# Two MLP pieces behind the last attention outputs, and one cast ahead of a silu, in a fused attention and MLP kernel

## The chip, the core and the metric

The kernel runs on one core of a Trainium2 chip. The metric is the device time of one execution in microseconds (us); it was 192.3 us before the change (median of 3 runs). Engines are named as in the profile: PE is TensorE (PEld its weight loads), DVE VectorE, ACT ScalarE, POOL GpSimd, SP SyncE, which here only issues DMAs.

## The reference

A linear attention with decay (RWKV5) over 4 batches, 8 heads, 768 steps and a head width of 48, followed by a two-layer MLP over the 3072 tokens. Cut to what is computed:

```python
for t in range(S):
    cur = einsum('bhd,bhe->bhde', u * k[t], v[t])
    y[t] = einsum('bhd,bhde->bhe', r[t], state + cur)
    state = w * state + einsum('bhd,bhe->bhde', k[t], v[t])
x = y.transpose(0, 2, 1, 3).reshape(3072, 384)
h = x @ w_in                  # 384 -> 2048
out = (h * sigmoid(h)) @ w_out    # 2048 -> 384
```

Inputs and output are float32.

## The kernel before

**Tiling.** The 768 steps are cut into 6 chunks of 128. A unit is one chunk of one batch: unit i has chunk i // 4 and batch i % 4, 24 units in all, worked on in pairs (i, i+1). Within a chunk the attention is matrix products: the tile T turns r and k of a unit (transposes on PE, L251), `decay_one` multiplies them with powers of w into rT and kT (DVE, L259), `product_halves` forms the products of kT and rT (PE, L351, name P), `masked_halves` masks them (DVE, L358, m), `sums` adds up k times v for the state (PE, L374, Q) from kc, a decayed copy of k, and v16, a 16-bit copy of v made by `cast_v` (ACT, L242). `state_first` (DVE L387, then casts s1h on ACT, L332) and `state_second` carry the state on. `outputs_halves` (PE, L424 and L433, Z) makes the outputs of a pair from rT16, a 16-bit copy of rT, the states and the masked products; `evict_halves` adds the bonus term and writes y16 (DVE, L305).

**The MLP.** It runs over chunks of 4 x 128 tokens. `turn_y_dma` turns y16 into xT by a DMA transpose on SP's queue (L455). A first-layer piece (`l1_mm`, L477, and `l1_silu`, L485 on ACT) makes 128 of the 2048 hidden columns for 512 tokens: three matmuls and a silu. A second-layer piece (`l2_mm`, L498) is four of the sixteen matmuls that make 128 tokens' outputs; after every fourth piece `store` copies the sums (ACT, L504) and SP writes them out (L508). First-layer pieces of a chunk need xT of all four of its units.

**Order.** Nothing is left to a scheduler: the instructions of each engine stand in the order of the code. The start is a list of words written out by hand (`order`, from L577). There a word L4.11 is the matmuls of a first-layer piece of chunk 0 and G4.11 its silu, v165 is `cast_v` of unit 5, T5, rT5 and kT5 turn and decay unit 5, Q4 P4 s1_4 m4 s2_4 Z4 z4 are the steps of the pair (4, 5), yT and xT turn y on PE and copy it on ACT, ku, ru, kc, vu, sd are POOL's products, and i_q and i_o are POOL's DMAs that load a group of the MLP's weights (`ld_win`, L83, `ld_wout`, L88). Group 3 of the first weights, which L4.12 and later pieces read, is loaded by i_q3.

From unit 6 on a loop (L610) goes over the pairs 6, 8, ..., 22. MLP pieces wait in a list, `fillers`, and `fill(n)` plays the next n of them between the attention's steps. A pair plays 4 (L626) between its sums and its outputs, 4 (L639) after the turns of the next pair, 2 ahead of each of two `cast_r`, and 4 (L647) at its end, 16 in all. The second pair of a chunk adds that chunk's 16 first-layer and 16 second-layer pieces to the list, right after its outputs. What is left is played behind the loop. In the last pair (22, 23) there is no next pair to turn; its outputs are turned by DMA and are followed by the second-layer pieces of chunk 4 that are left (7 of them), and then by the first layer of chunk 5.

PSUM has four banks for the MLP pieces, sums and outputs (tag `moe`, four buffers); a new tile takes over one of the four banks and waits for the last reader of the tile that held it.

Of the kernel before, what the change touches and what calls it, by code (L numbers as in the profile page):

```python
# [15 lines left out]
def kernel(  # L16
# [23 lines left out]
    NU = B * NCH  # L40
# [9 lines left out]
    def unit(i):  # L50
        return divmod(i, B)
# [24 lines left out]
    def load(i):  # L76
        if i >= NU:
            return
        for dst, src in ((rin, r), (kin, k), (vin, v)):
            ld(i, dst, src)  # L80
# [131 lines left out]
    def bonus_products(i):  # L212
        bonus_ku(i)
        bonus_rku(i)
# [10 lines left out]
    def decayed_k(i):  # L225
        nc.gpsimd.tensor_tensor(out=kc[i % NIN][:, :, 0:D], in0=kin[i % NIN][:, :, 0:D],  # L226
                                in1=lamH if unit(i)[0] else lamC, op=ALU.mult)

    def bonus_sum(i):
        L(i)["rku"] = wrk.tile([128, H], FP, name="rku")  # L230
        nc.vector.tensor_reduce(out=L(i)["rku"], in_=L(i)["rku_f"],  # L231
                                axis=mybir.AxisListType.X, op=ALU.add)

    def bonus_v(i):
        L(i)["vu"] = wrk.tile([128, H, D], FP, name="vu", bufs=4)
        nc.gpsimd.tensor_tensor(out=L(i)["vu"], in0=vin[i % NIN],  # L236
                                in1=L(i)["rku"].unsqueeze(2).broadcast_to([128, H, D]),
                                op=ALU.mult)
# [24 lines left out]
    def turn(i):  # L263
        turn_one(i, 0)
        turn_one(i, 1)

    def decay(i):
        decay_one(i, 0)
        decay_one(i, 1)
# [72 lines left out]
    def product_halves(i):  # L342
        a = next_att().rearrange("p j (e g c) -> p j e g c", e=2, g=NP)
        L(i)["a2"] = a
        for p in range(NP):
            for e in range(2):
                rT, kT = L(i + e)["rT"], L(i + e)["kT"]
                for x in range(2):
                    o0 = HC * x
                    for j, r0 in ((0, 0), (1, 64)):  # L350
                        nc.tensor.matmul(a[o0:o0 + HC, j, e, p, :],  # L351
                                         kT[r0:r0 + D, p, HC * x:HC * x + HC],
                                         rT[r0:r0 + D, p, HC * x:HC * x + HC],
                                         start=True, stop=True)

    def masked_halves(i):
        am = L(i)["am2"] = wrk.tile([128, 2, 2, NP, HC], F16, name="am")
        nc.vector.tensor_tensor(  # L358
            out=am.rearrange("p j e g c -> p (j e g) c"),
            in0=L(i)["a2"].rearrange("p j e g c -> p (j e g) c"),  # L360
            in1=maskH.unsqueeze(1).broadcast_to([128, 2 * H, HC]), op=ALU.mult)

    def sums(i):
        sc, b = unit(i)
        xs = range(2 if sc < NCH - 1 else 1)
        L(i)["sp"] = [ps.tile([128, 512], FP, name="sp", tag="moe", bufs=4) for _ in xs]
        for p in range(NP):
            for e in range(2):
                for x in xs:
                    rows = slice(HC * x, HC * x + HC)  # L370
                    for j in range(2):
                        h = 2 * p + j
                        c0 = (e * NP + p) * D
                        nc.tensor.matmul(L(i)["sp"][x][64 * j:64 * j + 64, c0:c0 + D],  # L374
                                         kc[(i + e) % NIN][rows, h, :],
                                         L(i + e)["v16"][rows, h, :],
                                         start=True, stop=True)
# [7 lines left out]
    def state_first(i):  # L385
        s1 = L(i)["s1"] = wrk.tile([PR, 2, NP, D], FP, name="s1")
        nc.vector.tensor_tensor(out=flat(s1), in0=L(i)["sp"][0][0:PR, 0:HD],  # L387
                                in1=flat(L(i)["sdec"]), op=ALU.add)
        spread_state(nc.scalar.copy, inner[i // 2 % 2], s1)

    def state_second(i):
        sc, b = unit(i)
        if sc == NCH - 1:
            return
        sd = wrk.tile([PR, 2, NP, D], FP, name="sd")
        nc.vector.tensor_tensor(out=sd, in0=L(i)["s1"], in1=w_half(), op=ALU.mult)
        nc.vector.tensor_tensor(out=flat(st[b // 2]), in0=L(i)["sp"][1][0:PR, 0:HD],
                                in1=flat(sd), op=ALU.add)
# [6 lines left out]
    def next_state(i):  # L405
        sc, b = unit(i)
        if sc == NCH - 1:
            return
        spread_state(nc.gpsimd.tensor_copy, carried_in(i + B), st[b // 2])
        decayed_state(i + B)  # L410

    def outputs_halves(i):
        yp = L(i)["y2"] = [ps.tile([128, 512], FP, name="yp", tag="moe", bufs=4)
                           for _ in range(2)]

        def place(e, x, c0, n):
            y0 = rows(e, x)
            return yp[e][y0:y0 + HC, c0:c0 + n]

        for p in range(NP):  # L420
            for e in range(2):
                for x in (e, 1 - e):
                    s = inner[i // 2 % 2] if x else carried_in(i)
                    nc.tensor.matmul(place(e, x, PW * p, PW),  # L424
                                     L(i + e)["rT16"][:, p, HC * x:HC * x + HC], s[:, e, p, :],
                                     start=(p == 0), stop=False, skip_group_check=True)
        for p in range(NP):
            for j in range(2):
                h = 2 * p + j
                for e in range(2):  # L430
                    for x in range(2):
                        r = HC * x
                        nc.tensor.matmul(place(e, x, D * h, D), L(i)["am2"][r:r + HC, j, e, p, :],  # L433
                                         L(i + e)["v16"][r:r + HC, h, :],
                                         start=False, stop=True, skip_group_check=True)

    def evict_halves(i):
        yp = L(i)["y2"]
        new_y(i)
        add_bonus(i, yp[0])  # L440
        new_y(i + 1)
        for x in range(2):
            y0 = rows(1, x)
            add_bonus(i + 1, yp[1], slice(HC * x, HC * x + HC), slice(y0, y0 + HC))
# [8 lines left out]
    def turn_y_dma(i):  # L453
        sc, b = unit(i)
        nc.sync.dma_start_transpose(out=x_tile(sc)[:, :, b, :],  # L455
                                    in_=L(i)["y16"].rearrange("p h d -> p (h d)"))
# [81 lines left out]
    def fill(n):  # L538
        for _ in range(n):
            if fillers:  # L540
                fillers.pop(0)()

    def second(sc):
        return [lambda b=b, p=p: l2(sc, b, p) for b in range(B) for p in range(4)]

    def rest_first(sc):
        return [lambda ft=ft: l1(sc, 2, 2, ft) for ft in range(0, NFT, 2)]

    def first(sc):
        return [lambda f=f: l1(sc, 0, B, f) for f in range(NFT)]  # L550
# [5 lines left out]
    def piece(word, f):  # L556
# [24 lines left out]
        v163 4*A23 vu2 i_q2 rd3 vu3 am2 am3 L0.0 G0.0 L0.2 G0.2 Y2 y162 Y3 y163 kc0 yT2 xT2 L0.4  # L581
        G0.4 kc1 yT3 xT3 L0.6 G0.6 S0 st0 kc2 T4 kT4 rT4 kc3 L2.0 G2.0 L2.2 G2.2 ku4 v164
        L2.4 G2.4 S2 L2.6 G2.6 st2 ru4 i_q3 r164 L4.8 G4.8 L4.9 G4.9 rd4 ku5 kc4 kc5 sd4
        L4.10 G4.10 T5 kT5 rT5 L4.11 G4.11 vu4 ru5 i_o0 v165 Q4 P4 s1_4 m4 rd5 s2_4 r165
        L4.12 G4.12 vu5 i_o1 L4.13 G4.13 Z4 z4 L4.14 G4.14 L4.15 G4.15 yT4 xT4
        yT5 xT5 T6 kT6 rT6 kc6 ku6 ru6 i_o2 H0 H1 v166 r166 H2 H3 T7 kT7 rT7 kc7 ku7 i_o3 v167
        r167 H4 ru7 rd6 sd6 vu6 sn4
# [22 lines left out]
    for i in range(B + 2, NU, 2):  # L610
        sc, b = unit(i)
        nxt = range(i + 2, min(i + 4, NU))
        sums(i)
        product_halves(i)
        state_first(i)
        state_second(i)
        masked_halves(i)
        if i == B + 2:
            bonus_sum(i + 1)
            bonus_v(i + 1)  # L620
        for n in nxt:
            bonus_products(n)
            decayed_k(n)
        if i > B + 2 or sc < NCH - 1:
            next_state(i)
        fill(4)  # L626
        outputs_halves(i)
        for n in nxt:
            turn(n)
        evict_halves(i)  # L630
        turn_y_dma(i)
        turn_y_dma(i + 1)
        if b:
            fillers.extend((first(sc) if sc > 1 else rest_first(sc)) + second(sc))
        for n in nxt:
            decay(n)
        load(i + B)
        load(i + 1 + B)
        fill(4)  # L639
        for n in nxt:  # L640
            bonus_sum(n)
            cast_v(n)
            bonus_v(n)
        for n in nxt:
            fill(2)
            cast_r(n)
        fill(4)  # L647
    fill(len(fillers))


# [28 lines left out]
```

## Time and profile before

| | us |
|---|---|
| median of 3 runs (191.97 to 192.69) | 192.3 |
| profiled execution | 192.8 |
| its span, first to last instruction | 191.0 |
| PE busy | 180.1 (94%) |
| POOL busy | 118.6 (62%) |
| DVE busy | 114.7 (60%) |
| ACT busy | 99.0 (52%) |
| granted TensorE clock, mean | 0.997 |

The profiled execution is 0.5 us above the median, and 1.8 us of it lie outside its span. Places in time are us from the span's start. A row of the timeline gives the start, the length from the first to the last end of the merged instructions, the engine, line, operation, tiles and number, and in brackets the idle time of the engine ahead of it and what ended it. Matmuls overlap, so the length of a row of them is a little more than the distance to the next row.

### The profile page before, as it was taken

The numbers are of one execution on the slowest core, as the hardware profiler recorded it, in microseconds if no ns is written. First come the engines' busy times: TensorE is split into PE (matmuls) and PEld (weight loads), VectorE is DVE, ScalarE is ACT, GpSimd is POOL, SyncE is SP. The second block draws the span as 40 slices with busy tenths as digits, with TensorE's granted clock in tenths as the row PEclk, the third lists the DMA queues.
The fourth block names the chain that finished last, engine by engine and source line by source line (L and its number), as shares of the span: only waits on it lengthen the run. The fifth ranks groups of instructions, "written<-read, shape, count | busy, mean of one in ns | idle before, by whom it ended". The sixth has DMA issues, their size and how long they took to land. (4 is left out here: it accounts for less than half of the span.)

```text
span 191.0 us, 6511 instructions
## 1 busy us (share of the span) xinstructions
PE 180.1 (94%) x2786; PEld 113.1 (59%) x2786; DVE 114.7 (60%) x189; ACT 99.0 (52%) x193; POOL 118.6 (62%) x151
## 2 busy tenths in 40 slices
PE   7798898998999999999999999999999999999993
PEld 2454783677666786655656655656646566444562
DVE  7578876845884794695686775766853944200120
ACT  5394477576433293158573178563267643289200
POOL 6499989699899977849649649749659130000000
PEclk9999999999999999999999999999999999999998
DMA  5999979999959469269177269177386202310022
GB/s 95 209 191 189 207 149 184 155 218 222 148 113 195 148 134 200 65 129 223 26 147 165 65 138 209 32 146 165 84 177 163 41 4 82 85 42 0 6 79 84
DMA packets 90272, 24.42 MB, mean 128 GB/s; under 512 B 83329, under 2 KB 90242, under 8 KB 90242
## 3 DMA queue, kind: packets, MB, share of 16 engines
q1 hardware_dynamic: 84992, 20.39, 49.1%
q0 software_dynamic: 3712, 3.15, 10.8%
q10 hardware_dynamic: 1538, 0.46, 1.1%
q8 instruction: 22, 0.36, 0.8%
q14 instruction: 8, 0.07, 0.1%
HBM read 20.65 MB, written 4.72 MB: 133 GB/s over the span
## 5 line engine op out<-in xcount | busy, mean ns | idle before, releaser
L477 PE MATMUL hps<-xT,win 128*128 128x512 f16 (+1 forms) x360 | 66.4, 337 | 1.0 <-DMA xT<-y 0.5
L485 ACT ACTIVATE gT<-hps 128x512 f16<-128x512 f32 x96 | 55.8, 597 | 17.4 <-PE hps L477 14.2
L498 PE MATMUL ops<-wout,gT 128*128 128x384 f16 x368 | 62.5, 326 | 0.0
L477 PEld LDWEIGHTS <-win 128*128 128x128 f16 x360 | 33.8, 98 | 26.8 <-issue 1.6
L498 PEld LDWEIGHTS <-gT 128*128 128x128 f16 x368 | 35.2, 98 | 23.4
L236 POOL TENSOR_TENSOR vu<-vin,rku 128x384 f32<-128x384 f32 x24 | 21.1, 892 | 21.0 <-DVE rku L231 21.0
L218 POOL TENSOR_TENSOR ku<-kin,u_bc 128x384 f32<-128x384 f32 x24 | 24.4, 1018 | 11.1 <-DMA kin<-in_k_dram 7.5
L504 ACT COPY osb<-ops 128x384 f32<-128x384 f32 x20 | 9.6, 479 | 41.7 <-PE ops L498 31.1
L305 DVE TENSOR_TENSOR y<-yp,vu 64x384 f16<-64x384 f32 (+1 forms) x34 | 18.9, 555 | 13.7 <-PE yp L433 5.0
L222 POOL TENSOR_TENSOR rku_f<-rin,ku 128x384 f32<-128x384 f32 x24 | 24.3, 1012 | 1.7
L226 POOL TENSOR_TENSOR kc<-kin,lamH 128x384 f16<-128x384 f32 x20 | 20.7, 1038 | 0.0
L259 DVE TENSOR_TENSOR kT<-att,lamK 112x512 f32<-112x512 f32 x24 | 16.4, 683 | 4.8 <-PE att L251 4.8
L387 DVE TENSOR_TENSOR s<-sp,sdec 112x384 f32<-112x384 f32 x10 | 5.6, 558 | 22.0 <-PE sp L374 20.7
L259 DVE TENSOR_TENSOR rT<-att,lamR 112x512 f32<-112x512 f32 x24 | 16.5, 686 | 2.5 <-PE att L251 1.1
L332 ACT CAST s1h<-s 48x384 f16<-48x384 f32 x20 | 10.2, 511 | 9.6 <-DVE s L387 9.5
L242 ACT CAST v<-vin 128x384 f16<-128x384 f32 x24 | 11.5, 511 | 5.4 <-DMA vin<-in_v_dram 5.2
L506 DVE COPY osb<-ops 128x384 f32<-128x384 f32 x3 | 1.7, 558 | 20.6 <-issue 16.5
L273 DVE CAST rT<-rT 112x512 f16<-112x512 f32 x16 | 13.9, 906 | 0.0
L231 DVE TENSOR_REDUCE rku<-rku_f 128x8 f32<-128x384 f32 x24 | 12.5, 544 | 1.4 <-POOL rku_f L222 1.4
L358 DVE TENSOR_TENSOR am<-att,maskH 128x1024 f16<-128x1024 f32 x10 | 12.2, 1218 | 1.2 <-PE att L351 1.2
L351 PE MATMUL att<-rT,kT 48*64 48x64 f32 x640 | 11.6, 220 | 0.0
L251 PE MATMUL att<-ident,kin 64*112 64x64 f32 x192 | 9.4, 217 | 1.5 <-DMA kin<-in_k_dram 1.5
(74 smaller groups left out, 167.1 us busy)
## 6 DMA issues: line engine op xcount, KB each, us to landing
rin<-in_r_dram SPq DMA_DIRECT2D x24, 192.0 KB, 3.7
vin<-in_v_dram SPq DMA_DIRECT2D x24, 192.0 KB, 4.3
kin<-in_k_dram SPq DMA_DIRECT2D x23, 192.0 KB, 4.5
out_dram<-osb SPq DMA_DIRECT2D x23, 192.0 KB, 2.7
win<-in_moe_w_in_dram POOLq DMA_DIRECT2D x4, 384.0 KB, 6.5
wout<-in_moe_w_out_dram POOLq DMA_DIRECT2D x4, 384.0 KB, 6.2
xT<-y SPq DMA_TRANSPOSE x18, 2.3
kin<-in_k_dram ACTq DMA_DIRECT2D x1, 192.0 KB, 3.7
```

Source lines behind the costliest of these rows:

```text
L218: nc.gpsimd.tensor_tensor(out=L(i)["ku"], in0=kin[i % NIN][:, :, 0:D], in1=u_bc, op=ALU.mult)
L222: nc.gpsimd.tensor_tensor(out=L(i)["rku_f"], in0=rin[i % NIN][:, :, 0:D], in1=L(i)["ku"], op=ALU.mult)
L226: nc.gpsimd.tensor_tensor(out=kc[i % NIN][:, :, 0:D], in0=kin[i % NIN][:, :, 0:D], in1=lamH if unit(i)[0] else lamC, op=ALU.mult)
L231: nc.vector.tensor_reduce(out=L(i)["rku"], in_=L(i)["rku_f"], axis=mybir.AxisListType.X, op=ALU.add)
L236: nc.gpsimd.tensor_tensor(out=L(i)["vu"], in0=vin[i % NIN], in1=L(i)["rku"].unsqueeze(2).broadcast_to([128, H, D]), op=ALU.mult)
L259: nc.vector.tensor_tensor(out=L(i)[key].rearrange("p g (y t) -> p y g t", y=2), in0=L(i)["t"][0:PR, :, x], in1=lam, op=ALU.mult)
L273: copy(out=L(i)["rT16"], in_=L(i)["rT"])
L305: nc.vector.tensor_tensor(out=y16[a], in0=y[b, 0:HD], in1=vu[a], op=ALU.add)
L358: nc.vector.tensor_tensor(out=am.rearrange("p j e g c -> p (j e g) c"), in0=L(i)["a2"].rearrange("p j e g c -> p (j e g) c"), in1=maskH.un ...
L477: nc.tensor.matmul(hps[:, f, :], win[:, q, (ft + f) * 128:(ft + f + 1) * 128], xts[sc][:, q, b0:b0 + nb, :].rearrange("p b t -> p (b t)"), ...
L485: nc.scalar.activation(out=gts[sc][:, ft:ft + m, b0 * C:(b0 + nb) * C], in_=hpss[b0, ft], func=AF.Silu)
L498: nc.tensor.matmul(opss[b], gts[sc][:, ft, b * C:(b + 1) * C], wout[:, ft, :], start=(ft == 0), stop=(ft == NFT - 1))
```

## The change

Two edits. In the hand-written start, the cast of unit 5's v (v165) is moved on ACT's queue from behind the silu G4.11 (and behind POOL's i_o0 and ru5, to which it has no tie) to ahead of that silu. In the loop, the last `fill` of a pair plays 2 pieces in place of 4 from pair 20 on. For pair 20 that makes 14 pieces in place of 16; all later steps keep their numbers, so the two pieces come to stand behind the outputs of pair 22: nine second-layer pieces follow them in place of seven. For pair 22 itself it changes nothing, as the rest of the list is played right after. The order of POOL's instructions stays as it was. On SP's queue one store of chunk 4 moves from ahead of the last two DMA transposes to behind them, and on ACT one copy (L504) from ahead of the casts s1h of pair 22 to behind them.

```diff
-        L4.10 G4.10 T5 kT5 rT5 L4.11 G4.11 vu4 ru5 i_o0 v165 Q4 P4 s1_4 m4 rd5 s2_4 r165
+        L4.10 G4.10 T5 kT5 rT5 L4.11 v165 G4.11 vu4 ru5 i_o0 Q4 P4 s1_4 m4 rd5 s2_4 r165
...
         for n in nxt:
             fill(2)
             cast_r(n)
-        fill(4)
+        fill(4 if i < NU - 4 else 2)
     fill(len(fillers))
```

## The prediction

> **What bounds the kernel now.** I read the page's busy shares first, then the chain that ended last, then PE's waits in two stretches, then the timeline around each wait that the change touches.
>
> ```profile
> PE 180.1 (94%) x2786; PEld 113.1 (59%) x2786; DVE 114.7 (60%) x189; ACT 99.0 (52%) x193; POOL 118.6 (62%) x151
> ...
> PEclk9999999999999999999999999999999999999998
> ```
>
> PE is the bound: the other engines are busy at most 62% of the span and PE's clock is granted in full. The change adds and removes no PE work, so it can gain only idle time of PE. The chain that ended last, in order of time (start, length, what):
>
> ```profile
> 164.24 2.35 DMA xT<-y
> 166.59 0.14 issue
> 166.72 10.52 PE hps L477 x48
> 177.24 7.80 PE ops L498 x48
> ```
>
> The last transfer that turns y lands at 166.59, and behind it PE works through the first and second layer of the last chunk to the end. PE's own waits from 52 us to the end are a single row (waiter, releaser, total, times, longest), and from 28 to 52.5 us five:
>
> ```profile
> PE hps L477 <- DMA xT<-y: 0.5, 1, 0.5
> ```
>
> ```profile
> PE sp L374 <- ACT v L242: 1.1, 2, 0.9
> PE att L251 <- DMA kin<-in_k_dram: 0.5, 1, 0.5
> PE hps L477 <- DVE s L387: 0.5, 1, 0.5
> PE yp L424 <- ACT gT L485: 0.4, 1, 0.4
> PE yT L462 <- DVE y L305: 0.2, 1, 0.2
> ```
>
> So each edit aims at one wait: the pieces at the 0.5 us for xT, the cast at the 0.9 us for v16 of unit 5.
>
> **Edit 1, two pieces behind the last outputs.** PE's timeline there:
>
> ```profile
> 161.15 0.44 PE L433 MATMUL yp<-v,am 64*64 64x48 f16 x32
> 161.52 4.72 PE L498 MATMUL ops<-wout,gT 128*128 128x384 f16 x28
> 166.72 0.59 PE L477 MATMUL hps<-xT,win 128*128 128x512 f16 x2 [0.47 <-DMA xT<-y]
> ```
>
> 28 matmuls (seven pieces) take 4.72 us, 0.169 each, so a piece takes 0.67 and two take 1.35. Taken from ahead of the sums of pair 22, they let everything of that pair start 1.35 earlier: the outputs end at 160.17, the transposes land at 166.59 - 1.35 = 165.24. Nine pieces now last from 160.17 to 166.24, the same end as before, and xT has been there for 1.0 us. The idle 0.47 goes: gain 0.47.
>
> What else waits on pair 22, now that its cover is 1.35 shorter? From DVE's, ACT's and POOL's rows: rT16 of unit 23 is ready at 152.97 + 1.78 = 154.75 and is wanted at 160.69 - 1.35 = 159.34. The bonus term (POOL) ends at 154.47 and is wanted at 160.3. v16 ends at 153.12, wanted by the sums at 155.30. The chain that starts at the sums moves with them: the mask ran 158.14 to 159.36 and is wanted at 161.15, a slack of 1.8 that stays, because the four pieces between sums and outputs stay (16 matmuls, 2.77 us from 157.99, are the cover; without it the mask would cost PE about 1.0). The casts s1h end at 158.82 - 1.35 = 157.47, wanted at 159.34. The copy that now stands behind them on ACT (0.48) ends by 158.0; what waits for its bank is the second of the nine pieces, at 160.8. On SP's queue the store of one tile moves behind the two transposes; nothing waits for a store for the next 14 us, and the transposes have one transfer less ahead of them. The last copy of chunk 4 ends at about 166.8, and the bank it frees is wanted by the fourth first-layer piece, 166.24 + 3 x 0.66 = 168.2. All of this costs nothing. Bounds of edit 1: gain 0 (the wait reappears elsewhere) to 0.47; I take 0.47, since the nearest cover has 1.0 us to spare. Once the wait is gone nothing is late next: PE is bound by its own work from 52 us to the end.
>
> **Edit 2, the cast ahead of the silu.** ACT's and PE's rows:
>
> ```profile
> 29.92 1.57 ACT L485 ACTIVATE gT<-hps 128x512 f16<-128x512 f32 x3
> 32.21 0.60 ACT L485 ACTIVATE gT<-hps 128x512 f16<-128x512 f32 x1 [0.71 <-PE hps L477]
> 32.70 0.50 ACT L242 CAST v<-vin 128x384 f16<-128x384 f32 x1
> ```
>
> ```profile
> 32.10 0.22 PE L374 MATMUL sp<-v,kc 64*64 64x48 f16 x4
> 33.26 0.41 PE L374 MATMUL sp<-v,kc 64*64 64x48 f16 x28 [0.94 <-ACT v L242]
> ```
>
> v of unit 5 was issued at 24.23 and landed 5.1 us later, at 29.3. ACT is free from 31.49, so the cast (0.50) ends at 31.99, inside ACT's 0.71 idle, and G4.11 still starts at 32.21: no cost on ACT. On PE the sums of the pair run through at 32.10; locally 0.94 of idle goes.
>
> What is late next? P4 needs rT of unit 5, which DVE ends at 32.07 + 0.68 = 32.75, so PE stalls some 0.4 after the sums and P4 ends about 33.84 in place of 34.57: lead 0.73. L4.12 then needs weight group 3, issued at 27.41 and landed 6.7 later, at 34.1: its lead is only 0.4. But the outputs of the pair had waited 0.40 for G4.12, and ACT comes to that silu about 0.9 sooner, so PE gets the lead back there. DVE (mask, rku, state, y back to back from 34.75 to 39.2) and POOL (back to back from the bonus of unit 5, which waits for rku, at 36.53 to the state product at 45.89) run 0.7 earlier. So all three engines bring a lead of about 0.7 to unit 9's turn, where PE already waited for a load:
>
> ```profile
> 50.82 0.39 PE L251 MATMUL att<-ident,rin 64*112 64x64 f32 x8
> 51.67 0.44 PE L251 MATMUL att<-ident,kin 64*112 64x64 f32 x8 [0.46 <-DMA kin<-in_k_dram]
> ```
>
> k of unit 9 was issued at 43.7 and took 7.9 us to land, at 51.6. Neither end hangs on compute: SP's queue issues loads back to back from 40.3 to 47.6, and the sixteen DMA engines are full (DMA share 1.20 to 1.32 in every 2 us stretch from 38 to 50, and 0.29 from 52 to 54). PE will reach k's part of this turn near 50.5 and wait 1.2 us in place of 0.46. The lead is spent there, and from 52 us on everything stands as before.
>
> One thing can move that landing: the POOL instructions i_o1 to i_o3 sit in the chain that runs 0.7 earlier, and each loads 384 KB of weights on the other queue. The last of these was issued at 44.1 and landed 7.2 later, at 51.3, just ahead of k. While both queues have work the weights take more:
>
> ```profile
> q0 software_dynamic: 506, 0.38, 82.0%
> q1 hardware_dynamic: 1135, 0.21, 45.1%
> ```
>
> (47.5 to 50.5 us; packets, MB, share of 16 engines.) The same bytes go before k's last packet either way, and the engines are full, so I take 0 for the landing. Its bounds are 0.7 earlier (the weights' lead handed on in full) and, against me, 2.5 us later (one whole weight transfer put in front of it that was not there). Edit 2 is worth 0, between +0.7 and -2.5.
>
> The longer wait at unit 9's turn could cost more than itself through the clock. The trace grants 1.00 in the 2 us stretch from 32 to 34 that holds the 0.94 us idle, and 1.00 from 50 to 52, so I take no cost. The Trainium skill (TensorE: Matmul & The Clock Gate, What's actually happening) speaks against long PE waits: after an idle window of about 3.4 us the clock falls to half. By that rule 1.2 us is too short to trip it; had it tripped, a window at half clock would cost about 1.7 us, an estimate from that page alone.
>
> **Sum.** 0.47 + 0 = 0.47 of the profiled 192.8, that is 192.3, with a span of 190.5. The median stood 0.5 below the profiled execution; 192.3 - 0.47 gives 191.8, or -0.25%. A measurement of this kernel tells about 0.5% (0.96 us) from no change, so this falls within it.
>
> **Rivals.** (a) The load is not what holds 52 us: k of unit 9 lands 0.7 earlier with the weights, or is earlier anyway in executions without the profiler. Then both edits count, 0.47 + 0.7 = 1.2: 191.1 us, faster by 0.6%. For: only the last two of k's sixteen parts land after 51, when the DMA share has dropped to 0.2. Against: full engines up to then. (b) Slower: the weights push k of unit 9 back. Place: unit 9's turn; price: up to one weight transfer, the 2.5 us in which q0 dominates, less 0.47, so 194.3 us. It decides from a landing later than 51.62 + 0.47 + 0.96 = 53.05. For: the shares above. Against: the last weights already land before k, so no further bytes can get ahead. (c) Nothing: the wait for xT comes back as another of the same size at the last pair, 192.3. Against: 1.0 us of slack at the transposes, 1.8 at the mask.
>
> **Chances.** Forecast 0.71, (a) 0.15, (b) 0.07, (c) 0.07. The forecast and (c) lie within 0.5%, with 0.02 of the forecast's spread beyond it on the fast side: faster 0.17, same 0.76, slower 0.07. The three runs of before spread by 0.7, so the forecast alone reaches from 191.4 to 192.2. The range takes in (a) and most of (c): 191.0 to 192.5; (b) is left out.
>
> **What would show it.** Right: no wait of PE on xT near 166, the sums of pair 4 without a wait on v, PE's wait on k at unit 9's turn grown to about 1.2 us with its end still near 51.7, and the work behind it at unchanged places up to pair 22. Wrong: unit 9's turn ending below 51.2 (towards a) or above 52.5 (towards b), a wait at L424 or L433 of pair 22, or any new PE wait between 52 and 166 us.

## Result, and the profile after

The changed kernel is faster: median 191.38 us against 192.84 us before (20 executions of each; the 192.3 us ahead of the change is the median of the first three), ratio 0.9935 with a 95% interval of 0.9908 to 0.9962, that is 1.25 us (0.7 to 1.8). Ratios here and below leave out executions more than 1.5% above the fastest of their kernel, medians do not, so a ratio is not quite that of the medians. The forecast was 191.8 us and no measurable change; the time lies in the range, but at the place of rival (a), faster by 0.6%. The profiled execution took 190.8 us with a span of 189.0, 2.0 less than the one before.

The page after, busy shares and granted clock:

```profile
PE 179.4 (95%) x2786; PEld 112.8 (60%) x2786; DVE 115.0 (61%) x189; ACT 98.9 (52%) x193; POOL 118.7 (63%) x151
...
PEclk9999999999999999999999999999999999999999
```

The chain that ended last, its last long pieces in order of time (start, length, what):

```profile
158.92 5.96 PE ops L498 x36
164.87 10.36 PE hps L477 x48
175.23 7.80 PE ops L498 x48
183.03 2.65 PE ops L523 x32
```

Before, this chain began with the transfer that turns y; now PE's own work goes on behind it and the transfer is gone from its end. PE's waits after, first from 28 to 52.5 us, then from 52 us to the end:

```profile
PE hps L477 <- DVE s L387: 0.7, 1, 0.7
PE yT L462 <- ACT gT L485: 0.5, 1, 0.5
PE sp L374 <- ACT v L242: 0.2, 1, 0.2
```

```profile
PE yp L433 <- DVE am L358: 0.2, 1, 0.2
```

Both waits that the edits aimed at are gone. So is the wait on k of unit 9, which was forecast to grow. Behind 52 us one wait is new, that of L433 on the mask; ahead of it yT now waits for a silu where the outputs of pair 4 (L424) did before. The places, in PE's rows of the timeline after; first the last outputs and what follows them:

```profile
158.85 6.02 PE L498 MATMUL ops<-wout,gT 128*128 128x384 f16 x36
164.71 10.52 PE L477 MATMUL hps<-xT,win 128*128 128x512 f16 x48
```

36 matmuls, and then the first layer with no idle time in brackets. Next the sums of pair 4, on ACT and PE:

```profile
31.16 0.53 ACT L242 CAST v<-vin 128x384 f16<-128x384 f32 x1
...
31.89 0.44 PE L374 MATMUL sp<-v,kc 64*64 64x48 f16 x32
32.00 0.60 ACT L485 ACTIVATE gT<-hps 128x512 f16<-128x512 f32 x1 [0.31 <-PE hps L477]
```

The cast ends ahead of the sums, which are one row of 32 now, and the silu behind it still waits for PE, as worked out. Last, unit 9's turn:

```profile
49.83 0.39 PE L251 MATMUL att<-ident,rin 64*112 64x64 f32 x8
50.05 0.39 PE L251 MATMUL att<-ident,kin 64*112 64x64 f32 x8
```

k follows r with no wait. Why is seen on SP's queue, in the row that issues k of unit 9, before and then after:

```profile
43.73 0.62 SPq L72 DMA_DIRECT2D kin<-in_k_dram  x1
```

```profile
39.95 2.67 SPq L72 DMA_DIRECT2D kin<-in_k_dram  x1
```

and the time from this issue to its landing, from the answer on that tile after:

```profile
DMA to landing us min/median/max: 7.3/7.3/7.3
```

It was issued 3.8 us earlier and had landed at 47.3, where before it landed at 51.6. The cast can't have done that: SP's queue already stood one load further at 12 us, long ahead of the moved cast.

**Where the 2.0 us of span came from**, as the lead of the later trace over the earlier at the same step: 0.21 at the sums of pair 4 (32.10 to 31.89, before anything the change moves), 1.00 at unit 8's turn (50.33 to 49.33), 1.62 at k of unit 9 (51.67 to 50.05), 1.66 at the outputs of pair 8 (64.00 to 62.34), 1.38 at the sums of pair 10 and then without change up to pair 20 (142.87 to 141.50), 2.01 at the last chunk's first layer (166.72 to 164.71), 2.01 at the end. So the opening gave 0.21, the cast 0.79, the load's wait 0.66 with the outputs of pair 8, the new wait on the mask took 0.28, and the pieces gave 0.63.

### The profile page after: what moved, and what is told of

It is laid out like the page before. It is cut to its first block, busy times and chain, and to the rows that moved or that the text cites. A ratio compares the mean times of both kernels' runs of the same rounds, so it can differ in the third digit from the quotient of the medians.

```text
span 189.0 us, 6512 instructions
## 1 busy us (share of the span) xinstructions
PE 179.4 (95%) x2786; PEld 112.8 (60%) x2786; DVE 115.0 (61%) x189; ACT 98.9 (52%) x193; POOL 118.7 (63%) x151
## 4 chain that ended last, share of the span: by engine, by line
PE 71%; POOL 18%; issue 3%; DMA 3%; DVE 2%; ACTq 1%; ACT 0%; POOLq 0%; DVEq 0%
PE ops L498 31%; PE hps L477 26%; PE att L251 4%; POOL ku L218 4%; POOL kc L226 4%; PE att L351 4%; POOL rku_f L222 3%; POOL vu L236 3%; DMA u_bc<-in_u_dram 3%; PE yp L424 2%; PE yp L433 2%; PE sp L374 2%; POOL win L83 2%; PE ops L523 1%; POOL wout L88 1%
## 5 line engine op out<-in xcount | busy, mean ns | idle before, releaser
L485 ACT ACTIVATE gT<-hps 128x512 f16<-128x512 f32 x96 | 55.8, 597 | 18.9 <-PE hps L477 15.5
L504 ACT COPY osb<-ops 128x384 f32<-128x384 f32 x20 | 9.6, 478 | 40.3 <-PE ops L498 31.0
L305 DVE TENSOR_TENSOR y<-yp,vu 64x384 f16<-64x384 f32 (+1 forms) x34 | 18.9, 555 | 13.4 <-PE yp L433 5.6
L387 DVE TENSOR_TENSOR s<-sp,sdec 112x384 f32<-112x384 f32 x10 | 5.6, 557 | 19.2 <-PE sp L374 17.7
L242 ACT CAST v<-vin 128x384 f16<-128x384 f32 x24 | 11.4, 511 | 3.0 <-DMA vin<-in_v_dram 2.9
L351 PEld LDWEIGHTS att<-rT,kT 48*64 48x64 f32 x640 | 10.5, 135 | 0.2 <-DVE rT L259 0.2
## 6 DMA issues: line engine op xcount, KB each, us to landing
rin<-in_r_dram SPq DMA_DIRECT2D x24, 192.0 KB, 3.9
vin<-in_v_dram SPq DMA_DIRECT2D x24, 192.0 KB, 4.4
kin<-in_k_dram SPq DMA_DIRECT2D x23, 192.0 KB, 4.4
out_dram<-osb SPq DMA_DIRECT2D x23, 192.0 KB, 2.7
kin<-in_k_dram ACTq DMA_DIRECT2D x1, 192.0 KB, 3.5
```

What stands on the lines that cost most here:

```text
L305: nc.vector.tensor_tensor(out=y16[a], in0=y[b, 0:HD], in1=vu[a], op=ALU.add)
L351: nc.tensor.matmul(a[o0:o0 + HC, j, e, p, :], kT[r0:r0 + D, p, HC * x:HC * x + HC], rT[r0:r0 + D, p, HC * x:HC * x + HC], start=True, stop ...
L485: nc.scalar.activation(out=gts[sc][:, ft:ft + m, b0 * C:(b0 + nb) * C], in_=hpss[b0, ft], func=AF.Silu)
```

## The experiments

Each trace is read by stretches, since the opening ahead of the change moves much more than the change: the sums of pair 4 began between 31.9 and 36.3 us in the profiled executions of this case, whose instructions up to there differ only in the place of the cast and, in e12, of one weight load. All lengths are from the first matmul of one step to the first of another. "Pair 4 to k9" runs from the sums of pair 4 to k's part of unit 9's turn; "wait on k9" is the distance of k's part of that turn from unit 8's, less 0.45, which it is without a wait; "gap" is the distance between the last second-layer matmul ahead of the last chunk's first layer and that layer, less 0.16, which it is in an unbroken row; "k9 to end" goes to the last matmul.

| trace | cast ahead | pieces behind outputs | pair 4 to k9 | wait on k9 | gap | k9 to end |
|---|---|---|---|---|---|---|
| before | no | 7 | 19.57 | 0.62 | 0.64 | 135.79 |
| after | yes | 9 | 18.16 | 0 | 0 | 135.40 |
| e1_pieces | no | 9 | 18.94 | 0 | 0 | 135.39 |
| e2_cast | yes | 7 | 19.77 | 1.60 | 0.45 | 135.61 |
| e3_k9_first | no | 7 | 18.94 | 0 | 0.39 | 135.78 |
| e4_k9_first_cast | yes | 7 | 18.16 | 0 | 0.84 | 136.23 |
| e5_both_again | yes | 9 | 18.16 | 0 | 0 | 135.39 |
| e6_both_k9_first | yes | 9 | 18.14 | 0 | 0 | 135.40 |
| e7_k9_late | no | 7 | 20.40 | 1.44 | 0.37 | 135.52 |
| e8_k9_late_cast | yes | 7 | 20.68 | 2.50 | 0.69 | 137.52 |
| e9_cast_again | yes | 7 | 18.18 | 0 | 0.59 | 135.99 |
| e10_pieces_again | no | 9 | 18.96 | 0 | 0 | 135.74 |
| e11_fill6 | no | 5 | 18.96 | 0 | 2.14 | 137.53 |
| e12_q3_earlier | yes | 9 | 18.16 | 0 | 0 | 135.40 |

### One edit at a time

```diff
# e1_pieces, e10_pieces_again
-        fill(4)
+        fill(4 if i < NU - 4 else 2)
# e2_cast, e9_cast_again
-        ... L4.11 G4.11 vu4 ru5 i_o0 v165 Q4 ...
+        ... L4.11 v165 G4.11 vu4 ru5 i_o0 Q4 ...
```

**e1_pieces.** 

> Edit 1 alone (14 pieces in pair 20, so nine behind the last outputs; the cast of unit 5's v stays behind its silu). Theory A (PE idles 0.64 us start to start ahead of the last chunk's first layer, and nine pieces cover all of it): 0.6 us less than before, ratio 0.997; no wait of PE on xT near 166 us. Rival B (nearly the whole measured 1.25 us comes from this edit): 1.2 us less, ratio 0.9935. Rival C (the wait comes back at pair 22): no change.

Measured: 1.0005 (0.9970 to 1.0040), the time of before. In its trace the wait on xT is gone and from k9 to the end PE takes 135.39, which is 0.39 less than in e3_k9_first, the nearest trace with seven pieces. The stretch shows the mechanism of theory A, with 0.39 in place of 0.6, and excludes rivals B and C; the times exclude B, but can't resolve 0.4 us.

**e10_pieces_again**, the same kernel on another chip. 

> Edit 1 alone once more, on another chip. Theory A: 0.4 to 0.6 us less (the gap ahead of the last first layer measured 0.39 to 0.69 us beyond one matmul in the traces without the edit, and none in those with it), ratio 0.997 to 0.998. Rival C (no change): ratio 1.000 or above again.

Measured: 0.9994 (0.9967 to 1.0021). Again no gain to be seen in the time, and again no gap in the trace. But from k9 to the end this trace took 135.74, no less than e3: PE lost 0.35 within the outputs of pair 12, near 95 us, on nothing that the profile names. That PE has no gap is shown; that edit 1 alone makes the whole execution faster was not shown by these two comparisons, and the ratio that it should give, 0.997, lies at the lower edge of both intervals.

**e2_cast.** 

> Edit 2 alone (v of unit 5 is cast ahead of G4.11; pair 20 keeps 16 pieces). Theory A (PE, DVE and POOL gain 0.8 to 1.0 us by pair 6, and unit 9's turn hands most of it on because k of unit 9 has landed in most executions): 0.6 to 1.0 us less, ratio 0.995 to 0.997. Rival D, the step on record (k of unit 9 lands near 51.6 whatever the cast does, and takes the lead back): no change, with PE's wait on k at unit 9's turn near 1.2 us. In both PE's wait on v at the sums of pair 4 is gone and its wait on xT near 166 us stays.

Measured: 1.0012 (0.9976 to 1.0048), with executions from 191.3 to 195.1. Its profiled execution is the forecast's own case. The two longest of PE's waits from 28 to 54 us, and unit 9's turn:

```profile
PE att L251 <- DMA kin<-in_k_dram: 1.4, 1, 1.4
PE hps L477 <- DMA win<-in_moe_w_in_dram: 0.7, 1, 0.7
```

```profile
50.89 0.39 PE L251 MATMUL att<-ident,rin 64*112 64x64 f32 x8
52.72 0.44 PE L251 MATMUL att<-ident,kin 64*112 64x64 f32 x8 [1.44 <-DMA kin<-in_k_dram]
```

Here k of unit 9 landed 19.7 us after the sums of pair 4, in the trace before 19.5. The cast's lead is spent on that load to the last tenth: 19.77 from pair 4 to k9 with the cast, 19.57 without. L4.12 also waits for its weights, as foreseen.

**e9_cast_again**, on another chip. 

> Edit 2 alone once more, on another chip. Its first comparison gave 1.0012, with the load of k of unit 9 late in its profile (PE waited 1.4 us for it). Theory A (the lead counts when that load has landed, and how early it lands differs between executions and chips): somewhere from no change to 0.8 us less, ratio 0.996 to 1.000, with executions both near 191.5 and near 193.5. Rival H (edit 2 alone is worth nothing, and the two edits together do something that neither does): ratio 1.000 or above again, no fast group.

Measured: 0.9965 (0.9926 to 1.0003), six executions of 12 between 191.4 and 192.0. In its trace k of unit 9 had landed 16.1 us after the sums of pair 4, PE did not wait for it, and the stretch took 18.18. There is a fast group, which speaks for theory A and against rival H.

### The load taken out of the way

```diff
-    load(8)
-    load(9)
+    ld(9, kin, k)
+    ld(8, rin, r)
+    ld(8, kin, k)
+    ld(9, rin, r)
+    ld(8, vin, v)
+    ld(9, vin, v)
```

**e3_k9_first.** 

> The kernel before, with the loads of units 8 and 9 issued in another order: k of unit 9 first, then r and k of unit 8, r of unit 9, v of unit 8, v of unit 9 (same bytes). It takes the load out of unit 9's turn. Theory A (the load is late in some executions only): 0.2 to 0.4 us less, ratio near 0.9985, and the slower half of the executions comes closer to the faster. Rival D (the load is late in all executions): 0.5 to 0.7 us less, ratio 0.997. In both no wait of PE on k at unit 9's turn.

Measured: 0.9964 (0.9934 to 0.9994). No wait on k, 18.94 from pair 4 to k9: the same as in e1, e10 and e11, where the old order of loads did not make PE wait either. The interval holds what both theories expect; the traces decide for A.

**e4_k9_first_cast.** 

> The same new order of loads, with edit 2 (the cast ahead of G4.11) and without edit 1. With the load out of the way all theories say that the cast's lead is kept: against the same order of loads without the cast 0.8 to 1.0 us less (ratio to the kernel before 0.993 to 0.995). If it is less than 0.4, the lead is lost to something other than the load (a wait of DVE, POOL or PE between 34 and 52 us, or the mask of pair 8).

Measured: 0.9968 (0.9938 to 0.9998), no better than e3 in time, though the interval also holds part of what was expected. The stretch from pair 4 to k9 took 18.16, so the cast's lead, 0.78, is there up to unit 9. In this trace 0.45 of it went into a longer gap ahead of the last first layer (0.84, in e3 0.39): from the sums of pair 4 to the last matmul it took 154.39, and e3 154.72. Why the gap was longer, and why the times of these 12 executions show nothing, was not found.

**e6_both_k9_first**, both edits with that order. 

> Both edits with the new order of loads (k of unit 9 first). Theory A: both leads are kept in all executions, so 1.2 to 1.7 us less than before, ratio 0.991 to 0.994, and at or below the changed kernel. Rival F (the load order costs elsewhere what it saves, or the lead is lost at the mask of pair 8): no better than the changed kernel.

Measured: 0.9911 (0.9867 to 0.9954), median 191.35, beside 0.9930 of the changed kernel in the same comparison: the lowest ratio of the study, but not told apart from the changed kernel's. Its trace has the 18.14 and no gap.

**e5_both_again**, the changed kernel once more. 

> The changed kernel itself, once more, beside the kernel before on one chip. Theory A (edit 1 is worth 0.64 us in every execution; the cast's lead of about 0.8 us at unit 9's turn counts only where k of unit 9 has landed by then): 0.6 to 1.4 us less, ratio 0.993 to 0.997. Rival E (the opening before the change, which moves by 1 to 3 us from execution to execution, made most of the first comparison's 1.25 us): ratio 0.997 or above.

Measured: 0.9930 (0.9892 to 0.9968), the first result again, against another 23 executions of before. Rival E falls, if narrowly: the gain is not the opening's.

### The load made late

```diff
     load(8)
-    load(9)
+    ld(9, rin, r)
+    ld(9, vin, v)
+    for b in range(2):
+        spare = big.tile([128, H, D], FP, name=f"spare{b}")
+        nc.sync.dma_start(out=spare, in_=v[b, :, 0:C, :].rearrange("h t d -> t h d"))
+    ld(9, kin, k)
```

**e7_k9_late.** 

> The kernel before with k of unit 9 made late on purpose: its load is issued last of the six, behind two more loads of 192 KB into spare tiles that nothing reads. All theories: PE waits 1.5 to 3 us on it at unit 9's turn, ratio 1.005 to 1.012. It is the base for the next kernel.

**e8_k9_late_cast.** 

> The same late load with edit 2 (the cast ahead of G4.11). The step on record (the load takes the lead back) says: the same time as with the late load alone, within 0.2 us, and PE's wait on k longer by 0.7 to 1.0 us. Rival G (the lead reaches the end by another way, through DVE or POOL): 0.7 us or more less than with the late load alone.

Measured: 1.0104 (1.0050 to 1.0158) for the late load, and 1.0183 (1.0103 to 1.0263) with the cast, median 198.4 against 195.1 us (six executions each). Up to unit 9's turn the step on record holds: 20.40 without the cast, 20.68 with it, and PE's wait on k longer by 1.06. Rival G falls. But the cast made this kernel no faster, rather slower (the two intervals overlap), and the trace shows where time was lost. PE's row at unit 9's turn, and then 2 us stretches behind it (length, busy time and instructions of PE, PEld, DVE, ACT, POOL, granted clock, DMA share, GB/s):

```profile
55.55 0.44 PE L251 MATMUL att<-ident,kin 64*112 64x64 f32 x8 [2.34 <-DMA kin<-in_k_dram]
```

```profile
54.00:56.00 2.00, 0.46 (x9) 0.39 (x10) 1.52 (x3) 0.00 (x0) 1.92 (x3) 1.00 0.32 62
56.00:58.00 2.00, 2.00 (x7) 0.91 (x8) 1.75 (x3) 0.00 (x0) 1.92 (x3) 0.51 0.47 93
58.00:60.00 2.00, 2.00 (x9) 1.03 (x8) 1.84 (x3) 0.25 (x1) 1.94 (x4) 0.63 1.11 220
60.00:62.00 2.00, 2.00 (x15) 1.18 (x13) 0.00 (x0) 1.16 (x3) 1.92 (x4) 1.00 1.02 205
```

After a wait of 2.34 us PE's clock went to half, and came back within the stretch from 58 to 60 us: 7 and 9 matmuls started in 2 us, then 15. From k9 to the outputs of pair 8 PE took 14.02 us in place of the 12.34 of e7, 1.7 more. After waits of 1.28 (e7), 1.44 (e2) and 1.97 us (e11, below) the clock stayed at 1.00. The Trainium skill (TensorE: Matmul & The Clock Gate, What's actually happening) puts the fall to half clock behind an idle window of about 3.4 us; the fall is seen here, after less idle time than that. Nor does the length of one wait decide alone: in the opening of e11 the clock went to half near 11 us with no wait of PE above 0.53 us in the 7 us before (e3, e7, e8 and e12 show the same fall there):

```profile
12.00:14.00 2.00, 2.00 (x9) 0.60 (x6) 1.98 (x3) 1.97 (x6) 1.47 (x3) 0.50 1.04 206
```

To its last matmul the profiled execution of e8 took 3.5 us more than that of e7: 1.2 in the opening, up to the sums of pair 4, 0.3 up to unit 9's turn, 1.7 at half clock, and 0.3 in the gap ahead of the last first layer.

### The pieces the other way, and an earlier load of weights

```diff
# e11_fill6
-        fill(4)
+        fill(4 if i < NU - 4 else 6)
# e12_q3_earlier (on e6_both_k9_first)
-        L4.0 ... L2.2 G2.2 ku4 v164 ... st2 ru4 i_q3 r164 ...
+        L4.0 ... L2.2 G2.2 i_q3 ku4 v164 ... st2 ru4 r164 ...
```

**e11_fill6.** 

> The kernel before with 18 pieces in pair 20 in place of 16, so that five follow the last outputs: edit 1 the other way round. Theory A (the pieces behind the outputs cover the transposes one for one): the gap ahead of the last first layer grows from 0.4 to 0.7 by two pieces, 1.3, to 1.7 to 2.0 us, and the time by 1.3 us, ratio 1.006 to 1.008. Rival C (the wait only changes place): no change.

Measured: 1.0076 (1.0048 to 1.0105), 1.5 us slower. PE's rows at the place:

```profile
162.99 3.42 PE L498 MATMUL ops<-wout,gT 128*128 128x384 f16 x20
168.38 0.81 PE L477 MATMUL hps<-xT,win 128*128 128x512 f16 x3 [1.97 <-DMA xT<-y]
```

Five pieces behind the outputs, and a gap of 2.14 in place of 0.37 to 0.84 with seven and none with nine. The pieces cover the transposes one for one, within the spread of the gap, and here the time shows it too. Rival C falls.

**e12_q3_earlier.** 

> Both edits and the new order of loads, and the weight load i_q3 issued two POOL products (2 us) earlier, ahead of ku4. In the run without this PE waited 0.9 us for that load at L4.12. Theory A: that wait is gone, and where it bound, the sums of pair 4 to unit 9's turn take 17.7 us in place of 18.1; 0 to 0.4 us less than without it, ratio to the kernel before 0.989 to 0.992. Rival I (the earlier weights push the loads of units 6 to 9 back, or the later products of unit 4 hold up its bonus term): a new wait on a load or on rku, and no gain.

Measured: 0.9917 (0.9887 to 0.9947), no better than e6. The wait for the weights is gone, but pair 4 to k9 takes 18.16 as before: where PE does not wait for weights it waits for the state s instead (0.7 us, the first row of the waits after), and s waits 1.5 us for POOL's product sdec. So the 0.78 of the cast is POOL's lead, not PE's, and an earlier load of weights can't add to it.

## Why the prediction was right or wrong

- **Edit 1, 0.47 us: right in mechanism, the term somewhat small.** The gap was 0.64 in the trace before when counted from start to start; the 0.47 in brackets leaves out the end of the last matmul ahead of it. Over the seven traces with seven pieces it is 0.37 to 0.84, in the mean 0.57; over the six with nine it is 0. None of the covers that were listed for pair 22 failed.
- **Edit 2, the local lead: right.** The cast went into ACT's idle time at no cost, P4 stalled for rT of unit 5 on DVE, and the lead at unit 9 was forecast as 0.7; it is 0.78 (18.94 to 18.96 without the cast in four traces, 18.14 to 18.18 with it in six, where no load was waited for). In e2, e6, e8 and e9 L4.12 did wait for weight group 3, by 0.65 to 0.91, and as forecast this lead was got back.
- **Edit 2, "I take 0 for the landing": the step that failed.** That the load takes the lead back is true where the load is late; e2 and e8 show it. That it is late was read from one execution and taken for the rule. With the old order of loads k of unit 9 landed 11.4 to 19.7 us after the sums of pair 4, and PE wants it 18.9 us after them without the cast and 18.2 with it; it was waited for in two of eight traces, the one before and e2. In five of the other six (11.4 to 16.3 us) it came early enough for the cast to be worth its 0.78; in e1 it came at 18.55, which would have left about half. The step rested on "The same bytes go before k's last packet either way", and that does not hold. In the trace before, the last weights landed at 51.3, just ahead of k at 51.6. In the trace after, they were issued at 43.10 and took 7.2 us, to 50.3, and k had landed 3 us ahead of them. Their row on POOL's queue and the answer on that tile after:

```profile
43.10 0.81 POOL L88 DMA_DIRECT2D wout<-in_moe_w_out_dram  x1
```

```profile
DMA to landing us min/median/max: 7.2/7.2/7.2
```

  In the two traces in which PE waited, the last weights landed 0.4 us ahead of k; in the other six k landed ahead of them, by 0.5 us (e1) to 5.5 us (e5). Full engines do not fix which of the two comes first; k was issued at 43.73 in one trace and 39.95 in the other, and SP's queue had been one load apart since 12 us. What sets that pace is open. So is whether it changes with the execution or with the chip: e1 and e2 (18.6 and 19.7 us) ran on one chip, and e5 and e9 to e11 (11.4 to 16.3 us) on two others, with one trace of each.
- **The sum.** Where the load is late neither before nor after, the stretches give 0.57 + 0.78 = 1.35, which fits the 1.25 us measured (0.7 to 1.8). The forecast's 0.47 lies below that interval and was right for an execution with a late load only. That 191.38 us lies within the range all the same is no merit of the sum: the range had been drawn to take in rival (a). Rival (a) had the mechanism and the number, 1.2 us, and was given 0.15; its "earlier anyway" was the case to weigh.
- **"From 52 us on everything stands as before": wrong by 0.3 us.** Wherever k9 was not waited for, with the edits or without, PE lost about 0.28 at the outputs of pair 8 on the mask. The rows of DVE that precede it, before and after:

```profile
61.02 1.22 DVE L396 TENSOR_TENSOR sd<-s,wHT 112x384 f32<-112x384 f32 x1
```

```profile
59.35 1.89 DVE L396 TENSOR_TENSOR sd<-s,wHT 112x384 f32<-112x384 f32 x1
...
63.09 0.44 PE L433 MATMUL yp<-v,am 64*64 64x48 f16 x32 [0.22 <-DVE am L358]
```

  Over the fourteen traces the same product took 0.55 to 1.90 us. Where one of POOL's products ku, rku_f or kc was running when it began, with 0.15 us or more left, it ended 0.41 to 0.42 us behind the end of that one. In the ten traces with the new wait it began beside the POOL product vu, which ku followed, and ended 0.41 to 0.42 us behind the end of ku. The additions of L387 and L397, with one input in PSUM, took 0.55 to 0.56 us every time. The Trainium skill (SBUF — State Buffer, Who interferes with whom) says that a DVE instruction with two SBUF inputs contends with a POOL instruction that reads SBUF; these rows agree, but no run here took the POOL product away, so the cause is argued and not shown.
- **The clock.** The row of 1.00 held for the waits that occurred. That half a clock would cost about 1.7 us was met by e8, where the clock fell behind a longer wait, one still shorter than the rule asks for.
- **Left open.** Edit 1 alone, twice, and the cast with the new order of loads did not show in the times what their stretches show; each of these comparisons has an interval of 0.27% or more to either side. So the split of the gain between the edits rests on the traces: by the times alone, that the edits do more together than apart (rival H) is spoken against by e9 only.

## What to carry to other kernels

A load that is waited for by half a microsecond in one profile is a near miss, not a bound: before it is allowed to absorb a gain, its landing has to be set against the step that wants it in more than one execution. Compare traces by the same stretch between two steps, so that an opening that moves by microseconds drops out; the stretch from pair 4 to k9 repeated here to 0.04 us where no load was waited for, while the times of whole executions spread by 2 us and more. And an engine's idle time ahead of a long row is counted from start to start, not from the end that the profile draws.

## What the runs showed of the hardware

Behind a PE wait of 2.34 us the granted clock stood at half for 3.4 us, which cost 1.7 us (e8); behind waits of 1.28, 1.44 and 1.97 us it stayed at 1.00 (e7, e2, e11). A single wait is not the measure, though: in e11's opening the clock fell to half with no PE wait above 0.53 us in the 7 us before. The DVE product of L396, with both inputs in SBUF, took 0.55 to 1.90 us, and where it met a POOL product with 0.15 us or more left it ended 0.41 to 0.42 us behind that one. The landing of one and the same load moved by 8 us against compute from trace to trace (11.4 to 19.7 us after the sums of pair 4), to either side of the last weight load on the other queue.
